# Reordering a batched attention and maxout kernel: the second input batch ahead of the weights, and G pieces formed in the iteration that uses them

## The chip, the cores and the metric

The kernel runs on one core of one Trainium2 chip. The metric is the device time of one execution in microseconds (us). On one core a run counts as slow when it is over 1.5% above the fastest of the same kernel on that chip; such runs are left out of the ratios (with an exception, told at its place). Ratios here are the mean time of one kernel's fast runs over that of the other's fast runs of the same rounds, so they are not quite the ratio of the medians that stand beside them. Where 95% intervals are given, they belong to those ratios.

## The reference

A cross attention between 8 batches of x (8 heads, 512 rows of 64) and a small state (32 rows of 64), in both directions, feeds a maxout layer. All inputs are float32.

```python
def _attn_ref(x, state):
    scale = 1.0 / np.sqrt(D)
    a = softmax(scale * x @ state.T)            # 512 x 32 per head (max and 1e-09 left out here)
    xread = a @ state
    a2 = softmax(scale * state @ x.T)           # 32 x 512 per head
    sread = a2 @ x
    return np.concatenate([xread, sread], axis=2)

def _moe_ref(x, w1, w2, w3, w_out):             # x: 4352 x 512 here, w: 512 x 768, w_out: 768 x 512
    h = np.maximum(np.maximum(x @ w1, x @ w2), x @ w3)
    return h @ w_out
```

(The five lines of softmax are shortened to words.) Since xread @ w equals a @ (state @ w), the kernel forms G = state @ W for each batch once, in six column pieces, and multiplies the attention by G: a batch's maxout m needs piece m of G.

## The kernel before

Batches, pieces and maxouts are counted from 0. TensorE works in the program's order, so where a call stands in the text is where its matmuls stand on the engine, and the traces list them in that order. All PSUM (the matmuls' output memory) is held by two rotating sets: four one-bank buffers with the tag "pw", and two two-bank buffers with the tag "two", which scores and G pieces share. The third user of "two" in a row waits until the first user's reader is done.

```python
pp = ctx.enter_context(tc.tile_pool(name="pp", bufs=2, space=bass.MemoryType.PSUM))
# ...
def scores(b, g0, g1):
    if n == 2: p = pp.tile([128, J, n, HS, Ns], F32, tag="two", name="ps")   # whole batch
    else:      p = pp.tile([128, J, n, HS, Ns], F32, tag="pw", bufs=4, name="psh")
    # ... 16 (or 8) matmuls into p
    nc.scalar.activation(out=e[b][:, :, g0:g1], in_=p, func=AF.Exp, scale=scale)

def softmax(b, g0, g1, mul):      # VectorE: sum, reciprocal; mul: product, on VectorE or GpSimd
# ...
def a_transpose_dma(b):           # transposed attention aT by a DMA
    nc.sync.dma_start_transpose(out=aT[b]..., in_=a[b]...)

def g_cols(b, ms, copies=(nc.scalar.copy, nc.scalar.copy), defer=(False, False)):
    for m, copy, wait in zip(ms, copies, defer):
        p = pp.tile([128, 2, 512], F32, tag="two", name="pg")
        # ... 8 matmuls of state and W into p, then copy p into G[b]

def maxout(b, m, n, lhs, rhs, nk):
    for i in range(3):
        p = pp.tile([128, 512], F32, tag="pw", bufs=4, name=f"pw{i}")   # 2 matmuls each
    # ...
    nc.scalar.copy(out=t0[:, 0:n], in_=pw[0][:, 0:n])                   # "t" on ScalarE
    nc.vector.tensor_max(t1[:, 0:n], t0[:, 0:n], pw[1][:, 0:n])
    nc.vector.tensor_max(ht[b][:, m, :], t1[:, 0:n], pw[2][:, 0:n])

def ffn_out(b, j):                # output block: 6 matmuls into a "pw" buffer, copied by ScalarE
```

W is loaded by GpSimd's queue in four chunks (pieces 0, 1, 2 and 3, 4 and 5), each of three loads (w1, w2, w3). The loads are issued by the same engine that computes one of the softmax products. The loop, with the next batch n = b + 1 prepared behind the maxouts of batch b (cut):

```python
for b in range(2, B):
    if n < B:
        slots[0].append(lambda: scores(n, 0, 2))
        slots[1].append(lambda: softmax(n, 0, 2, nc.gpsimd.tensor_mul))
        slots[1].append(lambda: g_cols(n, (0, 1)))
        slots[2].append(lambda: a_transpose_dma(n))
        slots[3].append(lambda: sread(n))
        slots[3].append(lambda: g_cols(n, (2, 3)))
        slots[5].append(lambda: g_cols(n, (4, 5)))
        # ... and, every other batch, the states of two later batches: a transposing DMA, GpSimd copies
    for m in (1, 2, 4, 5):
        if pending: slots[m].append(lambda t=pending.pop(0): ffn_out(*t))
    for m in range(NM):
        x_maxout(b, m)
        for f in slots[m]: f()
```

Of the kernel before, what the change touches and what calls it, by code (L numbers as in the profile page):

```python
# [15 lines left out]
def kernel(  # L16
# [68 lines left out]
    for b in range(B):  # L85
        nc.gpsimd.memset(x_sb[b][:, XW:XW + D], 1.0)
# [5 lines left out]
    def load_w(c):  # L92
        m0, m1 = chunks[c]
        for i, w in enumerate((moe_w1, moe_w2, moe_w3)):
            nc.gpsimd.dma_start(  # L95
                out=w_sb[c][:, :, i, :],
                in_=w.rearrange("(kk p) f -> p kk f", p=128)[:, :, m0 * 128:m1 * 128])
# [6 lines left out]
    load_w(0)  # L104
    bds = [data.tile([128, 2, H, 2, Ns], BF16, name=f"bd{k}") for k in range(B // 2)]
    nc.vector.memset(bds[0], 0.0)
    load_x(1)
    load_w(1)
# [215 lines left out]
    both = (True, True)  # L324
# [11 lines left out]
    load_w(2)  # L336
    scores(0, 1, 2)
    softmax(0, 1, 2, nc.vector.tensor_mul)
    g_cols(0, (0,))
    load_w(3)  # L340
    load_x(2)
    keep_busy(4)
    a_transpose(0, 0, act)
    a_transpose(0, 1, dve)
    load_st(1, nc.scalar)
    x_maxout(0, 0)
    x_transpose(1, 0, act)
    x_transpose(1, 1, dve)
    sread(0)
    scores(1, 0, 2)  # L350
    softmax(1, 0, 2, nc.vector.tensor_mul)
# [3 lines left out]
    load_x(3)  # L355
    states_cast(1, pool)
    g_cols(0, (1,))
    g_cols(1, (0,), defer=both)
    x_maxout(0, 1)
    a_transpose(1, 0, act)  # L360
    a_transpose(1, 1, dve)
    g_cols(0, (2, 3), (act, dve))
    x_maxout(1, 0)
    x_maxout(0, 2)
    g_cols(1, (1, 2), defer=both)
    x_maxout(0, 3)
# [3 lines left out]
    x_maxout(1, 1)  # L370
    g_cols(0, (4, 5), defer=both)
    x_maxout(1, 2)
    scores(2, 0, 2)
    softmax(2, 0, 2, nc.gpsimd.tensor_mul)
    a_transpose_dma(2)
    x_transpose_dma(3)
    x_maxout(0, 4)
    g_cols(1, (3, 4), defer=both)
    sread(1)
    x_maxout(0, 5)  # L380
    g_cols(1, (5,))
    g_cols(2, (0,), defer=both)
    x_maxout(1, 3)
    ffn_out(0, 0)
    g_cols(2, (1, 2), (act, dve), defer=both)
    x_maxout(1, 4)
# [5 lines left out]
    g_cols(2, (3, 4))  # L392
    sread(2)
    ffn_out(0, 2)
    g_cols(2, (5,))
# [3 lines left out]
    pending = [(1, j) for j in range(J)]  # L399
    for b in range(2, B):  # L400
        n = b + 1
        slots = [[] for _ in range(NM)]
        if n < B:
            slots[0].append(lambda: scores(n, 0, 2))
            slots[1].append(lambda: softmax(n, 0, 2, nc.gpsimd.tensor_mul))
            slots[1].append(lambda: g_cols(n, (0, 1)))
            slots[2].append(lambda: a_transpose_dma(n))
            slots[3].append(lambda: sread(n))
            slots[3].append(lambda: g_cols(n, (2, 3)))
            slots[5].append(lambda: g_cols(n, (4, 5)))  # L410
            slots[4].append(late_transposes)
            if n + 1 < B:
                slots[0].append(lambda: x_transpose_dma(n + 1))
            if n % 2 and n + 1 < B:
                slots[2].append(lambda: states((n + 1) // 2, pool))
            if n + 2 < B:
                slots[0].append(lambda: load_x(n + 2))
        else:
            for m in range(NM):
                slots[m].append(lambda m=m: s_maxout(m))  # L420
        for m in (1, 2, 4, 5):
            if pending:
                slots[m].append(lambda t=pending.pop(0): ffn_out(*t))
        for m in range(NM):
            x_maxout(b, m)
            for f in slots[m]:
                f()
        pending += [(b, j) for j in range(J)]
    assert pending == [(B - 1, j) for j in range(J)]
# [36 lines left out]
```

## Time and profile before

| | before |
|---|---|
| median of the first 3 runs | 165.56 us (164.5 to 165.8) |
| span of the profiled run | 161.6 us |
| score of batch 3 starts (the loop's first) | 51.52 us |
| scores of batches 4 to 7 | 67.23, 82.94, 98.64, 114.72 us |
| first maxout of batch 2 starts | 50.22 us |

The scores are a good clock for the loop: they come once in a batch, so the distance of two is the loop's period (15.71 us), and what lies ahead of the first is the start. The page and the chain are shown in the prediction. Here are three lines of TensorE's waits; a line reads: the engine and the line that waited, what it waited for, then us in total, how many times, and the longest.

```profile
PE pg L249 <- ACT G L255: 2.3, 4, 0.8
...
PE pg L249 <- ACT e L181: 0.8, 1, 0.8
...
PE pg L249 <- DMA w<-in_moe_w_dram: 0.5, 1, 0.5
```

All of these lie in the start. W is hardly waited for (0.5 us), and the wait of a G piece for the exponential ("ACT e") happened once.

### The profile page before, as it was taken

Reading aid. Unit: us, or ns where it says so; the run is one execution under the profiler, and the core shown is the slowest. Engines: PE = TensorE matmul, PEld = TensorE weight load, DVE = VectorE, ACT = ScalarE, POOL = GpSimd, SP = SyncE. Lnnn points to the kernel's source line nnn. Section 1 sums busy time; section 2 is a strip of 40 time slices with the busy share of each in tenths; the row PEclk is TensorE's granted clock in tenths of the full one; section 3 lists DMA queues with packets and bytes.
Section 4 is the critical chain, followed back from the end, with each engine's and each line's share of the span. In section 5 each row is a group of like instructions: output and inputs, shape, how many; then the busy total and the mean of one; then the engine's idle time right before and its main releaser. Section 6 shows DMA issues by size and latency. Waiting matters only on the chain.

```text
span 161.6 us, 3531 instructions
## 1 busy us (share of the span) xinstructions
PE 149.4 (92%) x1417; PEld 70.8 (44%) x1417; DVE 95.8 (59%) x160; ACT 95.6 (59%) x153; POOL 48.0 (30%) x69
## 2 busy tenths in 40 slices
PE   7669799688999999999999999999999999999990
PEld 2336245243445443544344434443444366666440
DVE  4775788576572775576548663956394665585001
ACT  3354667758666936884687667675767653333440
POOL 8979520013063044606031334240123010100140
PEclk9999789999999999999999999999999999999999
DMA  4999999907739995599969639342305230030365
GB/s 120 206 166 195 197 197 211 204 6 38 163 130 132 185 219 106 186 197 231 176 185 139 57 73 274 119 111 94 134 0 154 53 130 2 0 130 4 130 218 171
DMA packets 37873, 21.99 MB, mean 136 GB/s; under 512 B 23009, under 2 KB 35553, under 8 KB 37857
## 3 DMA queue, kind: packets, MB, share of 16 engines
q0 software_dynamic: 17168, 14.94, 47.9%
q1 hardware_dynamic: 20400, 6.56, 22.0%
q10 hardware_dynamic: 288, 0.26, 0.6%
q8 instruction: 11, 0.18, 0.5%
q14 instruction: 6, 0.04, 0.1%
HBM read 15.20 MB, written 8.91 MB: 149 GB/s over the span
## 4 chain that ended last, share of the span: by engine, by line
PE 81%; ACT 8%; DVE 3%; DMA 3%; issue 2%; POOL 1%; SPq 0%; ACTq 0%; DVEq 0%; POOLq 0%
PE pw L270 41%; PE po L295 28%; PE pg L249 6%; ACT G L255 3%; DMA x0f<-in_x_dram 3%; PE psr L221 2%; ACT t L274 2%; PE ps L176 2%; ACT e L181 1%; DVE ht L278 1%; DVE xT L158 1%; PE pat L202 1%; POOL a L191 1%; ACT bd L139 0%; DVE x L331 0%
## 5 line engine op out<-in xcount | busy, mean ns | idle before, releaser
L270 PE MATMUL pw<-aT,G 128*128 128x512 bf16 x288 | 71.7, 384 | 0.9 <-DVE ht L278 0.5
L277 DVE TENSOR_TENSOR t<-t,pw 128x512 bf16<-128x512 bf16 (+1 forms) x54 | 35.1, 651 | 40.6 <-ACT t L274 37.2
L295 PE MATMUL po<-wout,ht 128*128 128x512 bf16 x204 | 48.7, 380 | 0.0
L270 PEld LDWEIGHTS <-G 128*128 128x128 bf16 x288 | 26.9, 98 | 34.5 <-issue 5.7
L255 ACT CAST G<-pg 128x768 bf16<-128x768 f32 x46 | 35.1, 803 | 10.4 <-PE pg L249 10.0
L278 DVE TENSOR_TENSOR ht<-t,pw 128x512 bf16<-128x512 bf16 (+1 forms) x54 | 35.5, 658 | 6.0 <-PE po L295 0.5
L274 ACT CAST t<-pw 128x512 bf16<-128x512 f32 (+1 forms) x54 | 30.6, 566 | 12.8 <-PE pw L270 11.4
L306 ACT COPY osb<-po 128x512 f32<-128x512 f32 x33 | 19.3, 586 | 25.5 <-PE po L295 25.2
L295 PEld LDWEIGHTS <-ht 128*128 128x128 bf16 x204 | 19.0, 98 | 23.8 <-issue 3.3
L315 POOL DMA_DIRECT2D out_dram<-osb x14 | 7.9, 566 | 55.0 <-ACT osb L306 54.3
L191 POOL TENSOR_TENSOR a<-e,rden 128x1024 bf16<-128x1024 bf16 (+1 forms) x7 | 12.5, 1784 | 38.2 <-DVE rden L190 29.1
L249 PE MATMUL pg<-w,bd 64*32 64x384 bf16 x384 | 13.5, 331 | 3.6 <-ACT G L255 2.3
L188 DVE TENSOR_REDUCE den<-e 128x32 f32<-128x1024 bf16 (+1 forms) x9 | 9.8, 1090 | 2.8 <-ACT e L181 2.8
L181 ACT ACTIVATE e<-ps 128x1024 bf16<-128x1024 f32 x7 | 7.2, 1024 | 5.4 <-PE ps L176 5.4
L249 PEld LDWEIGHTS <-bd 64*32 64x32 bf16 x384 | 3.9, 89 | 12.6 <-issue 11.2
L95 POOL DMA_DIRECT2D w<-in_moe_w_dram x12 | 9.0, 772 | 0.0
L270 PE MATMUL pw<-ats,w 128*128 128x256 bf16 x72 | 8.8, 273 | 0.0
L270 PEld LDWEIGHTS <-w 128*128 128x128 bf16 x72 | 7.0, 98 | 2.1
L139 POOL COPY bd<-stT 64x512 bf16<-64x512 bf16 x4 | 4.3, 1078 | 9.5 <-DMA stT<-st 9.4
L70 POOL DMA_DIRECT2D x<-in_x_dram x7 | 6.6, 944 | 1.5 <-DMA w<-in_moe_w_dram 1.2
L176 PEld LDWEIGHTS <-xT 128*128 128x128 bf16 x128 | 4.8, 98 | 3.4 <-DVE xT L158 1.0
L117 PE MATMUL idle<-zero 128*128 128x512 bf16 x13 | 4.6, 490 | 1.2 <-DVE zero L81 1.2
(43 smaller groups left out, 61.3 us busy)
## 6 DMA issues: line engine op xcount, KB each, us to landing
out_dram<-osb POOLq DMA_DIRECT2D x14, 512.0 KB, 3.4
x<-in_x_dram POOLq DMA_DIRECT2D x7, 512.0 KB, 7.4
w<-in_moe_w_dram POOLq DMA_DIRECT2D x6, 256.0 KB, 7.7
w<-in_moe_w_dram POOLq DMA_DIRECT2D x6, 128.0 KB, 5.5
wout<-in_moe_w_out_dram POOLq DMA_DIRECT2D x1, 768.0 KB, 14.1
x0f<-in_x_dram SPq DMA_DIRECT2D x1, 512.0 KB, 4.1
out_dram<-osb SPq DMA_DIRECT2D x1, 512.0 KB, 2.7
x<-in_x_dram POOLq DMA_DIRECT2D x1, 256.0 KB, 5.0
```

The costliest lines, as they stand in the source:

```text
L95: nc.gpsimd.dma_start(out=w_sb[c][:, :, i, :], in_=w.rearrange("(kk p) f -> p kk f", p=128)[:, :, m0 * 128:m1 * 128])
L181: nc.scalar.activation(out=e[b][:, :, g0:g1], in_=p, func=AF.Exp, scale=scale)
L188: nc.vector.reduce_sum(out=den, in_=e[b][:, :, g0:g1], axis=AX.X)
L191: mul(out=a[b][:, :, g0:g1].rearrange("p j g s n -> p j (g s) n"), in0=e[b][:, :, g0:g1].rearrange("p j g s n -> p j (g s) n"), in1=rden.r ...
L249: nc.tensor.matmul(p[32 * s:32 * s + 32, g, 0:384].rearrange("p (i f) -> p i f", i=3), bd(b, 2 * s + g)[64 * g:64 * g + 64, g, :], w[64 * ...
L255: copy(out=G[b][:, :, m * 384:(m + 1) * 384], in_=p[:, :, 0:384])
L270: nc.tensor.matmul(p[:, 0:n], lhs(i, k), rhs(k), start=(k == 0), stop=(k == nk - 1))
L274: nc.scalar.copy(out=t0[:, 0:n], in_=pw[0][:, 0:n])
L277: nc.vector.tensor_max(t1[:, 0:n], t0[:, 0:n], pw[1][:, 0:n])
L278: nc.vector.tensor_max(ht[b][:, m, :], t1[:, 0:n], pw[2][:, 0:n])
L295: nc.tensor.matmul(p, ht[b][:, m, j * 128:(j + 1) * 128], wout_sb[:, m, :], start=(m == 0), stop=(m == NM - 1))
L306: act(out=o[:, j, :], in_=p)
```

## The change

Its intent: fill the holes of the start by giving TensorE a second batch to work on early (x of batch 1 ahead of W, and its attention beside that of batch 0), and form pieces 2 to 5 of a batch's G in its own iteration rather than one iteration ahead. The diff, cut to its core:

```diff
-    for b in range(B):
-        nc.gpsimd.memset(x_sb[b][:, XW:XW + D], 1.0)
+    load_x(1)
 ...
     load_w(0)
+    load_w(1, (0,))
-    load_x(1)
-    load_w(1)
 ...
     softmax(0, 0, 1, nc.gpsimd.tensor_mul)
-    load_w(2)
+    load_w(1, (1, 2))
     scores(0, 1, 2)
     softmax(0, 1, 2, nc.vector.tensor_mul)
+    x_transpose(1, 0, act)
+    x_transpose(1, 1, dve)
     a_transpose(0, 0, act)
     a_transpose(0, 1, dve)
+    g_cols(0, (0,))
+    scores(1, 0, 1)
+    scores(1, 1, 2)
+    softmax(1, 0, 1, nc.gpsimd.tensor_mul)
+    load_w(2)
+    softmax(1, 1, 2, nc.vector.tensor_mul)
+    load_w(3)
 ...   # maxouts of batches 0 and 1 in another mix; then:
+    x_maxout(1, 3)
     scores(2, 0, 2)
+    ffn_out(0, 0)
+    x_maxout(1, 4)
+    softmax(2, 0, 2, nc.gpsimd.tensor_mul)
+    a_transpose_dma(2)
     ffn_out(0, 1)
     x_maxout(1, 5)
     sread(2)
+    g_cols(2, (0, 1))
     ffn_out(0, 2)
     ffn_out(0, 3)
 ...   # the loop
-            slots[1].append(lambda: g_cols(n, (0, 1)))
-            slots[3].append(lambda: sread(n))
-            slots[3].append(lambda: g_cols(n, (2, 3)))
-            slots[5].append(lambda: g_cols(n, (4, 5)))
+        slots[0].append(lambda: g_cols(b, (2, 3), (act, dve)))
+        slots[2].append(lambda: g_cols(b, (4, 5)))
+        if n < B:
+            slots[4].append(lambda: sread(n))
+            slots[4].append(lambda: g_cols(n, (0, 1)))
+        for j, m in enumerate((1, 2, 4, 5)):
+            slots[m].insert(0, lambda j=j: ffn_out(b - 1, j))
```

In slot 0 the G pieces stand right behind the score of the next batch; in slot 2 the output block comes first, and the G pieces stand right ahead of maxout 3.

More of the change, by code (lines that the diff above doesn't have):

```diff
@@ L90, with load_w @@
     wout_sb = wpool.tile([128, NM, d_model], BF16, name="wout")
-    def load_w(c):
+    def load_w(c, parts=(0, 1, 2)):
         m0, m1 = chunks[c]
-        for i, w in enumerate((moe_w1, moe_w2, moe_w3)):
+        for i in parts:
+            w = (moe_w1, moe_w2, moe_w3)[i]
             nc.gpsimd.dma_start(
@@ L104 @@
     load_w(0)
+    for b in range(B):
+        nc.gpsimd.memset(x_sb[b][:, XW:XW + D], 1.0)
+    load_w(1, (0,))
     bds = [data.tile([128, 2, H, 2, Ns], BF16, name=f"bd{k}") for k in range(B // 2)]
     nc.vector.memset(bds[0], 0.0)
-    load_x(1)
-    load_w(1)
     warm = const.tile([128, 1], F32, name="warm")
@@ L322, in late_transposes @@
             late.pop(0)()
-    both = (True, True)
     keep_busy(5)
@@ L335 @@
     softmax(0, 0, 1, nc.gpsimd.tensor_mul)
-    load_w(2)
+    load_w(1, (1, 2))
     scores(0, 1, 2)
     softmax(0, 1, 2, nc.vector.tensor_mul)
-    g_cols(0, (0,))
-    load_w(3)
-    load_x(2)
     keep_busy(4)
+    x_transpose(1, 0, act)
+    x_transpose(1, 1, dve)
     a_transpose(0, 0, act)
     a_transpose(0, 1, dve)
-    load_st(1, nc.scalar)
+    g_cols(0, (0,))
[5 more added lines that the diff above has]
+    load_w(3)
+    load_st(1, nc.gpsimd)
+    load_x(2)
     x_maxout(0, 0)
-    x_transpose(1, 0, act)
-    x_transpose(1, 1, dve)
+    g_cols(0, (1,))
+    g_cols(1, (0,))
     sread(0)
-    scores(1, 0, 2)
-    softmax(1, 0, 2, nc.vector.tensor_mul)
+    a_transpose(1, 0, act)
+    a_transpose(1, 1, dve)
+    x_maxout(0, 1)
     nc.gpsimd.dma_start(out=wout_sb, in_=moe_w_out.rearrange("(kk p) f -> p kk f", p=128))
@@ L355 @@
     load_x(3)
-    states_cast(1, pool)
-    g_cols(0, (1,))
-    g_cols(1, (0,), defer=both)
-    x_maxout(0, 1)
-    a_transpose(1, 0, act)
-    a_transpose(1, 1, dve)
-    g_cols(0, (2, 3), (act, dve))
-    x_maxout(1, 0)
-    x_maxout(0, 2)
-    g_cols(1, (1, 2), defer=both)
-    x_maxout(0, 3)
+    x_maxout(1, 0)
+    g_cols(0, (2, 3), (act, dve))
+    sread(1)
+    g_cols(1, (1,), defer=(True,))
+    x_maxout(0, 2)
+    x_maxout(1, 1)
+    g_cols(1, (2, 3), defer=(False, True))
+    x_maxout(0, 3)
+    states_cast(1, pool)
+    g_cols(0, (4, 5), defer=(False, True))
+    x_maxout(1, 2)
+    x_maxout(0, 4)
     states(1, act)
@@ L369 @@
     x_transpose(2, 1, act)
-    x_maxout(1, 1)
-    g_cols(0, (4, 5), defer=both)
-    x_maxout(1, 2)
+    x_maxout(0, 5)
+    g_cols(1, (4, 5), defer=(False, True))
+    x_maxout(1, 3)
+    x_transpose_dma(3)
     scores(2, 0, 2)
+    ffn_out(0, 0)
+    x_maxout(1, 4)
     softmax(2, 0, 2, nc.gpsimd.tensor_mul)
     a_transpose_dma(2)
-    x_transpose_dma(3)
-    x_maxout(0, 4)
-    g_cols(1, (3, 4), defer=both)
-    sread(1)
-    x_maxout(0, 5)
-    g_cols(1, (5,))
-    g_cols(2, (0,), defer=both)
-    x_maxout(1, 3)
-    ffn_out(0, 0)
-    g_cols(2, (1, 2), (act, dve), defer=both)
-    x_maxout(1, 4)
     ffn_out(0, 1)
@@ L391 @@
     x_maxout(1, 5)
-    g_cols(2, (3, 4))
     sread(2)
+    g_cols(2, (0, 1))
     ffn_out(0, 2)
-    g_cols(2, (5,))
     ffn_out(0, 3)
-    pending = [(1, j) for j in range(J)]
     for b in range(2, B):
@@ L403 @@
         if n < B:
+            if n + 1 < B:
+                slots[0].append(lambda: x_transpose_dma(n + 1))
             slots[0].append(lambda: scores(n, 0, 2))
             slots[1].append(lambda: softmax(n, 0, 2, nc.gpsimd.tensor_mul))
-            slots[1].append(lambda: g_cols(n, (0, 1)))
             slots[2].append(lambda: a_transpose_dma(n))
-            slots[3].append(lambda: sread(n))
-            slots[3].append(lambda: g_cols(n, (2, 3)))
-            slots[5].append(lambda: g_cols(n, (4, 5)))
-            slots[4].append(late_transposes)
-            if n + 1 < B:
-                slots[0].append(lambda: x_transpose_dma(n + 1))
             if n % 2 and n + 1 < B:
                 slots[2].append(lambda: states((n + 1) // 2, pool))
+            slots[5].append(late_transposes)
             if n + 2 < B:
@@ L420 @@
                 slots[m].append(lambda m=m: s_maxout(m))
-        for m in (1, 2, 4, 5):
-            if pending:
-                slots[m].append(lambda t=pending.pop(0): ffn_out(*t))
+        slots[0].append(lambda: g_cols(b, (2, 3), (act, dve)))
[5 more added lines that the diff above has]
+            slots[m].insert(0, lambda j=j: ffn_out(b - 1, j))
         for m in range(NM):
@@ L427 @@
                 f()
-        pending += [(b, j) for j in range(J)]
-    assert pending == [(B - 1, j) for j in range(J)]
     ffn_out(B - 1, 0)
```

## The prediction

> **What bounds the kernel now.** I read the page's shares first, then the span in 40 slices, then the chain that ended last, then the timeline around two places in it.
>
> ```profile
> PE 149.4 (92%) x1417; PEld 70.8 (44%) x1417; DVE 95.8 (59%) x160; ACT 95.6 (59%) x153; POOL 48.0 (30%) x69
> ...
> PE   7669799688999999999999999999999999999990
> ...
> PEclk9999789999999999999999999999999999999999
> ```
>
> TensorE is the bound on average, but the slices (4.04 us each) show two stages. Up to about 40 us TensorE has holes: in the stretches 0-10, 10-20, 20-30 and 30-40 us it is busy 6.90, 7.87, 9.09 and 7.92 us, so 8.2 us of the 40 are empty, and one stretch ran at a reduced clock (0.7 and 0.8 in slices 4 and 5). From 40 us to the end it is full. The chain says the same: until 39.15 us it jumps between DMA, VectorE, ScalarE and TensorE, and from there it is TensorE alone, save one 1.1 us step at 110 us. One batch of the steady loop, score to score:
>
> ```profile
> 67.39 0.47 PE ps L176 x16
> 67.86 1.29 PE pw L270 x6
> 69.15 0.45 PE pg L249 x16
> 69.60 1.40 PE po L295 x6
> ...
> 83.10 0.47 PE ps L176 x16
> ```
>
> The columns are start, length, what. The period is 83.10 - 67.39 = 15.71 us, and its TensorE pieces add up to that: six maxouts (pw) and four output blocks (po) of 1.29 us, three pairs of G pieces (pg) of 0.45, a score (0.47), a state read (0.56), and 0.07 to 0.11 at each change of shape. So in the loop any new wait of TensorE is lost one for one, and only the first 40 us have something to win.
>
> **What the Trainium skill says.** "PSUM — Partial Sum Buffer", Specifications (TRN2): eight banks of 2 KiB per partition. The kernel's two pools take four one-bank buffers ("pw": maxouts, output blocks, state reads, transposes) and two two-bank buffers ("two": scores and G pieces), all eight; a score and two G pieces therefore compete for two buffers. "Perfetto Trace Analysis", Identifying Performance Opportunities (Optimization Strategy): "Consistent bubbles" on the engine that should be saturated "can mean there isn't enough SBUF/PSUM for the next tile to be allocated". The trace before has it once, at 15 us:
>
> ```profile
> 14.98 0.90 PE L176 MATMUL ps<-bd,xT 128*128 128x64 bf16 x16
> ...
> 15.82 0.36 PE L249 MATMUL pg<-w,bd 64*32 64x384 bf16 x8
> 15.93 1.02 ACT L181 ACTIVATE e<-ps 128x1024 bf16<-128x1024 f32 x1 [1.00 <-PE ps L176]
> ...
> 17.00 0.36 PE L249 MATMUL pg<-w,bd 64*32 64x384 bf16 x8 [0.83 <-ACT e L181]
> ```
>
> A score and two G pieces in a row: the second G piece needs the score's buffer and stood 0.83 us until the exponential had read it. "ScalarE: Activation LUTs", What ACT_TABLE_LOAD costs: an ACTIVATE takes 186 ns + 0.833 ns per element with an immediate scale, and back-to-back ones overlap by about 93 ns. The trace agrees: 1.02 us for the exponential of 1024 elements (1.04 by the formula), 0.80 for one G copy of 768, and 1.50 for two in a row. "TensorE: Matmul & The Clock Gate", Part 1: the gate is at half or full clock, by windows of about 3.4 us; the dip in slices 4 and 5 fits, behind a poorly filled stretch.
>
> **The change, part by part.** The matmuls are the same; only places change. I read the order of the built programs engine by engine, with their waits.
>
> *Loop, score and G pieces.* Before: maxout 0, score of the next batch, maxout 1, then two G pieces. After: maxout 0, score, G pieces 2 and 3 at once. The changed program has on the second of them a wait for ScalarE, that of the 15 us case. Worked with the loop's durations: in the batch at 67.23 us the exponential starts 0.72 us after the score (67.95) and ends at +1.74; the second piece can start at about +1.79; TensorE gets there at 0.46 (score, start to start) + 0.23 (half a pair) = +0.69. Loss 1.10 us in each of the five iterations that still score a next batch (b = 2 to 6): 5.5 us. The 15 us case had 0.83, which would make 4.2.
>
> *Loop, G pieces 4 and 5.* After, they come right ahead of maxout 3, which is followed by maxout 4 with no output block between. Both copies are on ScalarE ahead of maxout 3's first copy (t). The like of it before, where an output block did follow and hid it:
>
> ```profile
> 75.38 0.52 PE L249 MATMUL pg<-w,bd 64*32 64x384 bf16 x16
> ...
> 75.81 1.50 ACT L255 CAST G<-pg 128x768 bf16<-128x768 f32 x2 [1.10 <-PE pg L249]
> 75.83 0.98 PEld L270 LDWEIGHTS <-G 128*128 128x128 bf16 x6 [0.31 <-issue]
> 75.83 1.47 PE L270 MATMUL pw<-aT,G 128*128 128x512 bf16 x6
> ...
> 77.19 0.60 ACT L274 CAST t<-pw 128x512 bf16<-128x512 f32 x1
> ```
>
> Here t started 1.36 us after its maxout and ended at +1.96, against +0.68 and +1.27 when no G copy is ahead (65.93, 66.61). After, the output block's copy is ahead too: it starts 0.20 after the G matmuls, then 0.48 for it and 2 x 0.69 for the two G copies, so t starts 2.06 and ends 2.65 after the G matmuls began, 2.20 after maxout 3 did. By the waits, maxout 4's second product needs t's buffer, and its third the one that VectorE's first max frees (+0.04, 0.69 long, +0.04: +2.97). TensorE is ready for the second at 1.40 + 0.43 = 1.83, stands 0.37 to 0.41, is ready for the third at 2.67 and stands 0.30. Loss 0.71, five times 3.6 us. In b = 7 the state maxout lies between; I put 0.45.
>
> *Loop, taken away.* Waits of 0.07 us beside pairs, about 0.4 in all.
>
> *Start.* x of batch 1 now lands ahead of W. In the 40 finer slices of the DMA view for 0-45 us the transfers move some 0.2 MB per us (176 to 210 GB/s); counted in bytes as they land, x1 is then 1.44 MB into the stream, about 9.4 us (before, its transposes ran at 13.27), and the first W piece 1.83 MB, about 11.4 (before, G waited for it until 8.92). The first transposed attention was only there at 10.7, and the first maxout began at 11.81. I walked the engines by hand with the rows' durations (0.69 us per VectorE max, 0.59 per ScalarE copy, 0.7 to 0.8 per G copy, 1.29 per maxout): first maxout 12.9 us, since VectorE now does batch 1's softmax ahead of its two maxes, which end at 17.5; the second waits for those buffers until 17.0; two of its successors follow by 19.8; then G pieces 2 and 3 stand until about 21.2 for the third W chunk, because GpSimd issues it only after the product for batch 1 at 15.4 (before it was issued from 10.63). From there maxouts of both batches alternate, VectorE paces them at about 1.4 us each, and the last output block of batch 0 ends at about 45.2 us. Before, the same work, with four G pieces of batch 2 (0.9 us) on top, ended at 50.39. That would be a gain of 50.39 - 0.9 - 45.2 = 4.3 us.
>
> But batch 2's softmax was moved behind maxout (1,4): sum 40.5, reciprocal to 42.0, GpSimd product (1.91) to 43.9, then the transposing DMA, 4.7 us from issue to landing for this batch before (issued at 37.76, long ahead of its use at 50.39). So maxout (2,0) starts at about 48.5: 3.3 us are given back, and 1.0 stays.
>
> **Sum.** 5.5 + 3.6 + 0.45 - 0.4 - 1.0 = +8.1 us; 165.56 + 8.1 = 173.7. The walk of the start is the loosest term and the 0.83 case says that the first could be 1.3 smaller, so I put 173.0.
>
> **Rivals.** (1) The start gains its full 4 us or more and the attention of batch 2 arrives in time, since GpSimd's and VectorE's places may fall earlier than my walk has them. For it: before, 8.2 us of holes lie there, and filling them is the change's intent. Against it: the softmax's place in VectorE's order is fixed behind ten maxouts' maxes. With full loop losses: 165.56 + 9.1 - 4.3 = 170.4. (2) Moving G pieces costs nothing, as TensorE's waits are covered: then only the start counts, 161 to 165. For it: ScalarE and VectorE are only 59% busy. Against it: the wait for the exponential is one of latency, seen at 0.83 us with ScalarE free. (3) The loop becomes ScalarE- or VectorE-bound: ScalarE has per batch 6 x 0.59 + 5 x 0.7 + 4 x 0.59 + 1.02 = 10.4 us, VectorE 12 x 0.69 + 2.0 of softmax and state read + 0.96 = 11.2, both well below 17.5, so no. (4) The start is worse: the 3.3 us hole and the thin stretch at 14-17 us let the clock gate close for a window or two more, each up to 1.7 us: 175 to 177.
>
> **Range and chances.** The loop losses are read off waits in the program and have a case in the trace: 6 to 10 us. The start is -4.5 to +2. Together 169.0 to 177.0. Within 2% (up to 168.9) asks for the smallest loss and the largest gain at once; faster asks for rival 2. Slower by over 2%: 0.88, within: 0.10, faster: 0.02.
>
> **What would show it.** Right: the loop's period, score to score, at about 17.5 instead of 15.71 us; on the G matmul a recurrent wait of about 1 us for the exponential, five times; waits of 0.3 to 0.4 on the maxout after pieces 4 and 5, for ScalarE's t and VectorE's max; batch 1's transposes at 9 to 10 us; maxout (2,0) waiting about 3 us for the transposing DMA. Wrong: a period below 16.2 us, or maxout (2,0) beginning before 46 us with no wait.

## The result

The changed kernel takes 179.4 us in the median of 4 runs (179.01 to 181.7), the kernel before 165.68 in 4 runs beside it (164.5 to 169.08). The ratio is 1.0876, with an interval of 1.0789 to 1.0963. The direction was right; the size was not: 173.0 was predicted, and 179.4 lies above the range of 169 to 177.

The page after (shares and instructions of the engines; then TensorE's busy tenths and granted clock in 40 slices of 4.4 us):

```profile
PE 153.0 (86%) x1397; PEld 72.2 (41%) x1417; DVE 100.9 (57%) x167; ACT 91.6 (52%) x149; POOL 49.6 (28%) x71
...
PE   7877549999947798979898999899899999999991
...
PEclk9999966999996999999999999999999999999999
```

TensorE's share fell from 92% to 86%. There are two things to see. Counted from 0, slices 4 and 5 are thin and so are 11 to 13, both with a reduced clock beside them. And from slice 14 to 28 there are 8s and 7s where before there was an unbroken 9. TensorE's waits name all of it:

```profile
PE pg L250 <- DMA w<-in_moe_w_dram: 4.4, 2, 4.1
PE pg L250 <- ACT e L182: 4.4, 5, 0.9
PE pw L271 <- DMA aT<-a: 3.6, 1, 3.6
PE pw L271 <- ACT t L275: 1.4, 5, 0.3
```

Two of these come five times, once for each iteration that still scores a next batch; two come in the start. I take the loop first. The chain that ended last, one batch from score to score (start, length, what):

```profile
74.69 0.48 PE ps L177 x16
75.25 1.03 ACT e L182
...
84.00 0.50 ACT t L275
84.52 0.70 DVE t L278
85.26 0.59 PE pw L271 x2
...
92.21 0.48 PE ps L177 x16
```

The period is 92.21 - 74.69 = 17.52 us, and the exponential, ScalarE's copy t and VectorE's first max of it have become links of the chain. The timeline of that batch (start, length, engine, line, operation, in brackets the idle time before it and what ended it):

```profile
75.25 1.02 ACT L182 ACTIVATE e<-ps 128x1024 bf16<-128x1024 f32 x1 [0.81 <-PE ps L177]
...
76.33 0.35 PE L250 MATMUL pg<-w,bd 64*32 64x384 bf16 x8 [0.89 <-ACT e L182]
...
82.49 1.51 ACT L256 CAST G<-pg 128x768 bf16<-128x768 f32 x2
...
83.87 1.11 ACT L275 CAST t<-pw 128x512 bf16<-128x512 f32 x2
...
84.54 1.31 PE L271 MATMUL pw<-aT,G 128*128 128x512 bf16 x4 [0.29 <-ACT t L275]
```

The second G piece starts at 76.33, just after the exponential that read the score has ended at 76.27. Maxout 4's second product (the x4 row at 84.54) stood 0.29 us until the first of the two t copies, that of maxout 3, was through, and that copy comes on the chain only at 84.00, where both G copies have ended (82.49 + 1.51). Its third product could have followed after the 0.43 us of the second, at 84.97; by the chain it started at 85.26, when VectorE's first max had ended.

In the start, TensorE's timeline:

```profile
9.86 1.07 PE L156 MATMUL pxt<-ident,x 128*128 128x128 bf16 x16 [0.49 <-DMA x<-in_x_dram]
...
24.49 0.84 PE L250 MATMUL pg<-w,bd 64*32 64x384 bf16 x16 [4.10 <-DMA w<-in_moe_w_dram]
...
54.20 2.72 PE L271 MATMUL pw<-aT,G 128*128 128x512 bf16 x6 [3.59 <-DMA aT<-a]
```

The first line is the intent fulfilled: x of batch 1 is transposed at 9.86 us, where before it was 13.27. The second is the G pieces 2 and 3 of batch 0, 4.10 us late for their W; they took 0.84 us instead of 0.52, and the maxout of batch 2 took 2.72 instead of 1.47: both ran at half clock (granted clock 0.50 from 24.5 to 26.7 and from 54.2 to 57.0 us). The timeline of GpSimd and of the SyncE queue says where those waits come from:

```profile
16.04 4.52 POOL L95 DMA_DIRECT2D w<-in_moe_w_dram  x6
...
47.31 1.91 POOL L192 TENSOR_TENSOR a<-e,rden 128x1024 bf16<-128x1024 bf16 x1 [17.95 <-DVE rden L191]
...
49.25 1.23 SPq L208 DMA_TRANSPOSE aT<-a  x1
```

W's third and fourth chunk are issued from 16.04 us on, since the program puts GpSimd's softmax product for batch 1 ahead of them. Before it was:

```profile
10.63 4.52 POOL L95 DMA_DIRECT2D w<-in_moe_w_dram  x6
```

Batch 2's product ends at 49.22, so that its transposing DMA lands only at 54.07.

The scores of batches 3 to 7 start at 56.72, 74.53, 92.05, 109.57 and 127.09 us. Between the two profiled spans, 161.6 and 177.4, there are 15.8 us: 5.20 come ahead of the first of these scores (56.72 against 51.52), and 10.63 behind it (120.68 to the end against 110.05). The medians differ by 13.7, because the profiled run of before, at 163.36 us, was faster than the median of its runs.

### The profile page after: what moved, and what is told of

It reads as the page before. It is cut to its first block, busy times and chain, and to the rows that moved or that the text cites. A ratio compares the mean times of both kernels' runs of the same rounds, so it can differ in the third digit from the quotient of the medians.

```text
span 177.4 us, 3523 instructions
## 1 busy us (share of the span) xinstructions
PE 153.0 (86%) x1397; PEld 72.2 (41%) x1417; DVE 100.9 (57%) x167; ACT 91.6 (52%) x149; POOL 49.6 (28%) x71
## 4 chain that ended last, share of the span: by engine, by line
PE 61%; ACT 11%; DMA 11%; DVE 6%; issue 5%; POOL 5%; ACTq 0%; POOLq 0%; DVEq 0%
PE pw L271 31%; PE po L296 21%; DMA w<-in_moe_w_dram 8%; PE pg L250 4%; ACT G L256 4%; ACT e L182 3%; DVE t L278 3%; DMA aT<-a 3%; ACT t L275 2%; PE psr L222 2%; PE ps L177 2%; POOL a L192 2%; POOL w L95 2%; ACT osb L307 1%; DVE ht L279 1%
## 5 line engine op out<-in xcount | busy, mean ns | idle before, releaser
L271 PE MATMUL pw<-aT,G 128*128 128x512 bf16 x288 | 74.0, 391 | 6.3 <-DMA aT<-a 3.6
L278 DVE TENSOR_TENSOR t<-t,pw 128x512 bf16<-128x512 bf16 (+1 forms) x54 | 35.1, 650 | 43.9 <-ACT t L275 34.7
L296 PE MATMUL po<-wout,ht 128*128 128x512 bf16 x184 | 46.6, 379 | 0.7
L256 ACT CAST G<-pg 128x768 bf16<-128x768 f32 x41 | 31.4, 804 | 11.0 <-PE pg L250 11.0
L296 PEld LDWEIGHTS <-ht 128*128 128x128 bf16 x204 | 19.8, 98 | 23.7 <-issue 0.3
L192 POOL TENSOR_TENSOR a<-e,rden 128x1024 bf16<-128x1024 bf16 (+1 forms) x8 | 13.5, 1690 | 56.2 <-DVE rden L191 44.5
L250 PE MATMUL pg<-w,bd 64*32 64x384 bf16 x384 | 14.3, 340 | 9.2 <-DMA w<-in_moe_w_dram 4.4
L256 DVE CAST G<-pg 128x768 bf16<-128x768 f32 x7 | 6.7, 957 | 8.5 <-PE pg L250 8.5
L250 PEld LDWEIGHTS <-bd 64*32 64x32 bf16 x384 | 4.0, 89 | 16.6 <-issue 15.8
L182 ACT ACTIVATE e<-ps 128x1024 bf16<-128x1024 f32 x6 | 6.1, 1024 | 5.2 <-PE ps L177 5.1
L118 PE MATMUL idle<-zero 128*128 128x512 bf16 x13 | 5.3, 554 | 1.2 <-DVE zero L81 1.2
```

The costliest lines, as they stand in the source:

```text
L192: mul(out=a[b][:, :, g0:g1].rearrange("p j g s n -> p j (g s) n"), in0=e[b][:, :, g0:g1].rearrange("p j g s n -> p j (g s) n"), in1=rden.r ...
L250: nc.tensor.matmul(p[32 * s:32 * s + 32, g, 0:384].rearrange("p (i f) -> p i f", i=3), bd(b, 2 * s + g)[64 * g:64 * g + 64, g, :], w[64 * ...
L256: copy(out=G[b][:, :, m * 384:(m + 1) * 384], in_=p[:, :, 0:384])
L271: nc.tensor.matmul(p[:, 0:n], lhs(i, k), rhs(k), start=(k == 0), stop=(k == nk - 1))
L296: nc.tensor.matmul(p, ht[b][:, m, j * 128:(j + 1) * 128], wout_sb[:, m, :], start=(m == 0), stop=(m == NM - 1))
```

## The experiments

My theory: the loop's two waits and the start's two waits make the whole loss, and each can be removed by moving a call. The rivals: the loop is slow for some other reason, such as G being formed late at all; the start costs what it does because of the low clock and not because of the waits; or behind a removed wait the next one stands at once. The edits below are against the changed kernel. The ratio against before is what can be compared.

| run | what it is | median us | ratio to before, 95% |
|---|---|---|---|
| a_oldloop | start of after, loop of before | 169.48 | 1.0340 (1.0262 to 1.0418) |
| b_oldstart | start of before, loop of after | 173.47 | 1.0581 (1.0509 to 1.0654) |
| c_w2early | third W chunk issued earlier | 173.95 | 1.0598 (1.0510 to 1.0685) |
| d_soft2early | softmax of batch 2 earlier | 174.0 | 1.0624 (1.0524 to 1.0725) |
| e_g23late / e_again | pieces 2, 3 behind maxout 1 | 175.17 / 174.73 | 1.0738 (1.0636 to 1.0840) / 1.0634 (1.0566 to 1.0701) |
| f_g45early / f_again | pieces 4, 5 ahead of the output block | 176.7 / 174.53 | 1.0769 (1.0677 to 1.0861) / 1.0607 (1.0524 to 1.0690) |
| g_all | c, d, e and f | 162.83 | 0.9937 (0.9867 to 1.0007) |
| h_busy / h_again | TensorE kept busy in both gaps | 178.28 / 178.54 | 1.0886 (1.0795 to 1.0977) / 1.0861 (1.0790 to 1.0932) |
| after_again | after, unedited | 179.82 | 1.0860 (1.0758 to 1.0963) |
| j_states0 | g_all, states earlier | 169.9 | 1.0275 (1.0183 to 1.0368) |
| k_oldstart_fixed | b with e and f | 164.9 | 1.0032 (0.9962 to 1.0102) |
| n_w3late | a gap between W chunks 3 and 4 | one look, 178.37 | state unknown |
| p_stsplit | g_all, states' DMA earlier | 161.56 | 0.9862 (0.9802 to 0.9922) |

### The two halves: a_oldloop and b_oldstart

The first undoes the loop, the second the start. The four G pieces of batch 2 that change sides were put where the loop needs them.

```diff
 # a_oldloop: start kept; loop of before, and
     ffn_out(0, 2)
+    g_cols(2, (2, 3))
     ffn_out(0, 3)
+    g_cols(2, (4, 5))
 # b_oldstart: everything ahead of the loop as before, but of batch 2 only pieces 0 and 1
-    g_cols(2, (1, 2), (act, dve), defer=both)
+    g_cols(2, (1,), (act,), defer=(True,))
 ...
-    g_cols(2, (3, 4))
-    g_cols(2, (5,))
```

(The second diff is against the kernel before.)

> Start of the changed kernel, loop of the kernel before (all of G formed an iteration ahead; batch 2's four later pieces behind its last output blocks, where TensorE waits anyway). Theory (start and loop are two separate losses, read off the two profiles: from the score in batch 2's iteration to the end 120.5 us after and 109.9 before): 179.4 - 10.6 = 168.8 us, period 15.7. Rival (the loop's loss comes with the late start, not with its order): above 175 us.

> Start of the kernel before without batch 2's G pieces 2 to 5, loop of the changed kernel. Theory: 165.6 + 10.6 - 0.9 (four pieces fewer in the start) = 175.3 us, period 17.5, the five waits for the exponential there. Rival (the loop's loss needs the new start): under 170 us.

The start alone costs 3.4%, the loop alone 5.8%; the sum, 9.2%, is close to the whole change's 8.8%. So the halves are nearly independent. In b the loop's period was 17.5 us (scores at 51.24, 68.71 and 86.23) at full clock, so the loop's loss needs neither the new start nor a low clock. In a, TensorE's waits for W (4.6 us) and for the transposed attention (3.0) stayed, and the last two periods are those of the kernel before, 15.71 us (88.94, 104.65, 120.36).

### The start's two waits: c_w2early and d_soft2early

```diff
 # c_w2early
     load_w(1, (1, 2))
+    load_w(2)
     scores(0, 1, 2)
 ...
     softmax(1, 0, 1, nc.gpsimd.tensor_mul)
-    load_w(2)
 # d_soft2early
     scores(2, 0, 2)
+    softmax(2, 0, 2, nc.gpsimd.tensor_mul)
+    a_transpose_dma(2)
     ffn_out(0, 0)
     x_maxout(1, 4)
-    softmax(2, 0, 2, nc.gpsimd.tensor_mul)
-    a_transpose_dma(2)
```

> Changed kernel, with the third W chunk's three loads issued ahead of GpSimd's product for batch 1. Theory (the place of the issue makes G pieces 2 and 3 of batch 0 stand 4.1 us, and the standing closes the clock gate): the wait falls to under 1 us and the half clock at 21 to 28 us goes with it, some 5 to 6.5 us, 173 to 174.4 us. Rival 1 (only the wait): 175.3 us with the half clock still there. Rival 2 (the transfers themselves are too slow, whenever issued): no change, 179 us.

> Changed kernel, with batch 2's softmax and its transposing DMA right behind its score, ahead of output block 0 and maxout (1,4). Theory (the wait of 3.6 us for the transposing DMA and the half clock after it come of the softmax's place): GpSimd's product starts at about 44.5 instead of 47.3, wait under 1 us, no half clock in batch 2: 179.4 - 3 - 1.7 = 174.7 us. Rival (VectorE's sum ahead of maxout (1,4) holds up TensorE as much as it gains): 177 to 179 us.

Each gained some 2.5% against the unedited 1.086 and 1.0876. The kernel before was 2.3 us faster than beside the unedited kernel, so the expected microseconds have to be read as ratios: c's 1.0598 lies between its theory (1.049 to 1.057) and its rival 1 (1.063), and its interval takes in both; d's 1.0624 is close to its theory (1.059). TensorE's timeline, first of c and then of d:

```profile
22.04 0.52 PE L250 MATMUL pg<-w,bd 64*32 64x384 bf16 x16
```

```profile
48.98 1.46 PE L271 MATMUL pw<-aT,G 128*128 128x512 bf16 x6 [0.92 <-DMA aT<-a]
```

In c the pieces 2 and 3 started at 22.04 us with no wait for W and at full clock (1.00 from 20 to 32 us, as the theory has it), while the wait for aT stayed at 3.6 us (its profile fell into a slow run of 177.32 us, so I read from it only the waits and this stretch). In d that wait fell from 3.6 to 0.9 us: the product started at 42.09 instead of 47.31, and the maxout of batch 2 at 48.98 instead of 54.20, with no half clock there. GpSimd had stood 17.95 us for this product, so only the place of the call held it back.

### The loop's two waits: e_g23late and f_g45early, each run twice

```diff
 # e: in the loop
-        slots[0].append(lambda: g_cols(b, (2, 3), (act, dve)))
 ...
             slots[m].insert(0, lambda j=j: ffn_out(b - 1, j))
+        slots[1].insert(0, lambda: g_cols(b, (2, 3), (act, dve)))
 # f: in the loop
-        slots[2].append(lambda: g_cols(b, (4, 5)))
 ...
             slots[m].insert(0, lambda j=j: ffn_out(b - 1, j))
+        slots[2].insert(0, lambda: g_cols(b, (4, 5)))   # ahead of the output block
```

In e maxout 1 runs while the exponential reads the score; in f the output block runs while the G pieces are copied.

> Changed kernel, with G pieces 2 and 3 of a batch moved from behind the next batch's score to behind maxout 1 (ahead of its output block). Theory (the second piece needs the score's PSUM buffer and waits for the exponential, 1.1 us in each of five iterations, nothing else there costs): the wait of pg for the exponential is gone, the period falls from 17.52 to 16.4 us, total -5.5 us, ratio to before 1.0876 - 0.033 = 1.054. Rival (the wait only moves: maxout 2 now waits for the copies of G, which come later): period stays above 17.2, ratio above 1.08.

> Changed kernel, with G pieces 4 and 5 moved from right ahead of maxout 3 to ahead of the output block before it. Theory (ScalarE's two G copies hold up the first copy of maxout 3, and so the PSUM buffers of maxout 4, for 0.71 us in five iterations and about 0.45 in the last): the waits of pw for ScalarE's t go, period 16.8 us, total -4.0 us, ratio about 1.063. Rival (VectorE's pace in two maxouts in a row makes the wait, whatever is ahead): under 1 us gained, ratio above 1.081.

The first pair gained less in time than expected, and the profiled execution of f ran at a granted clock of 0.659 throughout (227.9 us). So both were run again:

> The edit of e_g23late again (G pieces 2 and 3 behind maxout 1). Its profile showed the period at 16.4 to 16.8 us, its timed runs gained only 2.3 us. Theory (the loop's term is 5 times 0.9 to 1.1 us, and the start's scatter hid it): ratio 1.055 to 1.062 against 1.086 to 1.0876 unedited. Rival (a gain in the loop is lost elsewhere): 1.07 or above again, and the profile shows where.

> The edit of f_g45early again (G pieces 4 and 5 ahead of the output block), whose only profile fell into a run at 0.66 of the clock. Theory (0.71 us in five iterations, 0.45 in the last): no wait of pw for ScalarE's t, period 16.8, ratio 1.062 to 1.066. Rival (some 2 us, as the first three runs had it): 1.072 to 1.077, period 17.1 to 17.3.

The timeline of TensorE, first of e_again and then of f_again:

```profile
72.51 0.63 PE L177 MATMUL ps<-bd,xT 128*128 128x64 bf16 x16
...
74.36 0.52 PE L250 MATMUL pg<-w,bd 64*32 64x384 bf16 x16
```

```profile
79.20 2.75 PE L271 MATMUL pw<-aT,G 128*128 128x512 bf16 x12
```

In e both G pieces now run in one stretch of 0.52 us with nothing to wait for; in f maxouts 3 and 4 run through in 2.75. The clean periods were 72.51 to 88.95 = 16.44 us in e and 71.37 to 88.15 = 16.78 in f, against 17.52: 1.08 and 0.74 us less, where the prediction has 1.10 and 0.71. The times moved by 2.3% and 2.5% against the unedited kernel in the second pair, and by 1.2% and 0.9% in the first, where five waits of that size would make 3.3% and 2.3% of some 164 us. In the first pair e cannot be judged: its three timed runs (174.94 to 177.24) are all marked slow beside the profiled 171.61, and the ratio is the mean of these three; the one run marked fast would give 1.048. So f gave what was expected in the second pair only, and e fell short in the second. A part of that is in the profile: each edit brought one new wait of a score for GpSimd's state copies, of 0.59 and 0.75 us. The rest of it I have no run for.

### All four edits: g_all

> All four edits at once: third W chunk early, batch 2's softmax early, G pieces 2 and 3 behind maxout 1, G pieces 4 and 5 ahead of the output block. Theory (the four losses are separate and add): the ratios 1.0598 and 1.0624 of the first two runs and -0.033 and -0.024 for the others make 1.0876 - 0.028 - 0.025 - 0.033 - 0.024 = 0.978, period 15.7 us: faster than the kernel before by 2%. Rival (they share one wait, so that mending one opens another): 1.00 to 1.03.

It ran at 0.9937, between the theory's 0.978 and the rival's 1.00: with the four waits gone the loss is gone (the interval reaches 1.0007, and the clean periods are 15.71 us as before), but no clear gain over before remains. The start does gain: the score of batch 3 begins at 48.16 us, against 51.52 before, of which 0.9 are the G pieces that moved behind it. One of TensorE's new waits takes back a part:

```profile
PE ps L177 <- POOL bd L140: 1.3, 2, 1.2
```

GpSimd copies the states of later batches into place (bd) after a transposing DMA; the loop is now fast enough for the score to arrive before them. A second, of 1.2 us, was for x of batch 1 at the very start.

### Keeping the clock up: h_busy, and again as h_again

```diff
     x_maxout(1, 0)
+    keep_busy(18)
     g_cols(0, (2, 3), (act, dve))
 ...
     ffn_out(0, 3)
+    keep_busy(15)
```

These are idle matmuls into a "two" buffer in both gaps of the start. If the low clock costs time, filling the gaps should gain it, as long as nothing else moves.

> Changed kernel, with matmuls on zeros put where TensorE stands: 18 ahead of G pieces 2 and 3 of batch 0 (3.9 us at full clock), 15 ahead of batch 2's first maxout (3.2 us). The waits stay, only their filling changes. Theory (standing closes the clock gate, and the half clock of 6.8 and 3.4 us behind the two waits costs 0.5 us per us of work in it, some 3 to 4 us): clock 1.0 behind both waits, ratio about 1.066. Rival (the waits alone are the loss, or the gate follows something else): ratio 1.08 to 1.09.

> The run that fills TensorE's standing with matmuls on zeros, again: its clock was 1.0 and its time not better, while its one profile had the transposing DMA land 1.3 us later than all others. Theory (that was chance; the half clock does cost time): ratio 1.066 to 1.076. Rival (the clock is off the path that sets the end, or the fill costs what it gains): 1.083 to 1.09 again.

The clock was full, but no time was gained: 1.0886 and 1.0861 against 1.0876 and 1.0860. Here is the 20-30 us stretch of both (stretch, length, then busy us and count of TensorE, its weight loads, VectorE, ScalarE and GpSimd, granted clock, DMA share, GB/s), first of after:

```profile
20.00:30.00 10.00, 5.90 (x66) 2.23 (x65) 4.19 (x8) 2.24 (x4) 5.45 (x8) 0.66 1.37 191
```

and of h_again:

```profile
20.00:30.00 10.00, 8.23 (x87) 3.65 (x87) 4.57 (x9) 2.67 (x4) 5.53 (x8) 1.00 1.35 186
```

In h_again's trace the full clock did shorten what it touches: from G pieces 2 and 3 to the score of batch 2 it took 15.19 us instead of 16.77, and from the maxout of batch 2 to the score of batch 3 1.30 instead of 2.52, together 2.8 us less. But those G pieces started 1.5 us later (25.97 against 24.49): 0.6 of it because x of batch 1 had landed later, which happened ahead of any filler, and most of the rest because W took 9.25 us from the first issue to the G pieces instead of 8.45. And the transposing DMA for batch 2 took 6.16 us (49.15 to 55.31, where the maxout began), where it took 4.8 to 5.0 in every run of the new start without filler; h_busy's took 6.15. So in this trace the gain was eaten by transfers. I have no run that shows why they were slower. For the transposing DMA there is a candidate: the DMA view from 47 to 57 us of h_again has a line that no trace of the new start without filler (13 of them) has between this DMA's issue and its landing, and h_busy's has it too:

```profile
q8 instruction: 1, 0.02, 0.6%
```

This is one packet of the queue that the profile calls instruction. In both runs there are also some 1.5 us in this time in which all transfers together moved at most 14 GB/s. The fillers lengthen the program and may have brought this packet to this place; that is not shown, and in the kernel before, with such a packet at the same place, the DMA took 4.7 us.

How much time the half clock costs in the changed kernel is therefore not shown by the runs' times. The traces show a part: from the start of G pieces 2 and 3 to that of the score of batch 2, c_w2early took 15.03 us at full clock and h_again 15.02, against 16.61 in after, and in c the maxout of batch 2 came 28.13 us behind these pieces instead of 29.71. So the 1.6 us behind the first gap do reach batch 2's maxout. The second gap does not always lower the clock: in f_again the wait for aT was 3.61 us, and the maxout took 1.46. Of the six unedited runs of after_again, two took 177.26 and 177.89 us at a mean clock of 0.989 and 0.978, and four took 179.72 to 180.19 at 0.961 to 0.979. That fits a cost of about 2 us, but it is a correlation, and the one at 0.979 with 180.08 us is against it.

> The changed kernel itself, unedited, to have it beside the kernel before on the chip of the edited ones. Both theories: ratio 1.080 to 1.095. If it is near 1.089, filling TensorE's standing with matmuls gained nothing in all; if near 1.095 or above, it gained.

This run repeated the result: 1.0860 against 1.0876.

### Why the W loads came late: n_w3late

Here GpSimd writes a dummy tile eight times (4.6 us) between the third and the fourth W chunk, so that the third chunk's loads are alone in the queue.

```diff
     softmax(1, 1, 2, nc.vector.tensor_mul)
+    pad = const.tile([128, 512], BF16, name="pad")
+    for _ in range(8):
+        nc.gpsimd.memset(pad, 0.0)
     load_w(3)
```

> Changed kernel, with eight idle memsets on GpSimd (some 3 us in all) between the loads of the third and the fourth W chunk. Why did the third chunk land at 24.4 us and not at 21.2 as predicted? Theory (its last part shares the DMA engines with the fourth chunk's loads, issued right behind): it lands 1 to 1.5 us sooner, G pieces 2 and 3 start at about 23.2 us. Rival (the transfers only start slowly after standing from 15 to 17.5 us, and take turns in order): no change, 24.4 us.

It is one look at 178.37 us, of unknown state, and is used for its durations only. The timeline of GpSimd and TensorE in it:

```profile
17.03 2.29 POOL L95 DMA_DIRECT2D w<-in_moe_w_dram  x3
...
24.12 0.52 PE L250 MATMUL pg<-w,bd 64*32 64x384 bf16 x16 [2.73 <-DMA w<-in_moe_w_dram]
```

From the first issue to the G pieces it took 24.12 - 17.03 = 7.1 us, against 24.49 - 16.04 = 8.45 in after. The single loads took 4.1, 4.7 and 5.4 us from issue to landing, against 4.4, 4.9 and 6.8. By the clock the pieces came at 24.12, close to the rival's 24.4, but only because the issue was 1.0 us later. The shorter time fits the theory, yet it does not show that sharing makes the difference: e_g23late, whose start is unedited and whose fourth chunk follows at once, took 7.05 us (16.20 to 23.25), and the ten traces that issue both chunks in a row lie anywhere from 7.05 to 9.25. What makes this spread stays open. What all of them share is a slow start. The DMA view of after from 15 to 27 us, in slices of 0.3 us, shows their start:

```profile
GB/s 0 0 0 55 0 0 0 0 22 32 58 96 148 191 198 196 191 203 195 171 121 123 130 145 186 178 183 166 169 172 183 191 188 196 190 198 195 200 222 324
```

The loads begin in the slice at 17.4 us and reach the rate of the full queue only at 18.9, some 2.9 us after GpSimd began to issue them. With 0.79 MB at 0.2 MB per us, 3.9 us, that makes some 6.8 us (an estimate), about the shortest of the times above.

### Forming G late, by itself: k_oldstart_fixed

This is b_oldstart with the loop edits e and f, so that of the change only the place where G is formed is left.

> Start of the kernel before (without batch 2's G pieces 2 to 5), loop of the changed kernel with its two G pairs moved as in the two runs that did so. Theory (forming G within the iteration is neutral once the two waits are gone): 1.0581 - 0.033 - 0.024 = 1.001, period 15.7 to 15.9. Rival (it is worth something in itself, ScalarE and VectorE being evener): under 0.985.

At 1.0032 it is level with the kernel before: with the two pairs moved, forming pieces 2 to 5 in a batch's own iteration costs nothing that can be seen. Whether it would gain something is not shown, since the score waits for GpSimd's state copies (2.0 us in two waits, in a profile of a slow run) as in g_all; without them 1.0032 would become some 0.99, an estimate, still short of the rival's 0.985.

### The wait behind the waits: j_states0 and p_stsplit

The state copies consist of a transposing DMA and GpSimd copies behind it. j_states0 moves both from slot 2 to slot 0 of g_all; p_stsplit moves the DMA alone.

```diff
 # j_states0 (on top of g_all)
             slots[0].append(lambda: scores(n, 0, 2))
+            if n % 2 and n + 1 < B:
+                slots[0].append(lambda: states((n + 1) // 2, pool))
 ...
-            if n % 2 and n + 1 < B:
-                slots[2].append(lambda: states((n + 1) // 2, pool))
 # p_stsplit (on top of g_all): states_dma() holds the DMA, states() only the copies, left in slot 2
             slots[0].append(lambda: scores(n, 0, 2))
+            if n % 2 and n + 1 < B:
+                slots[0].append(lambda: states_dma((n + 1) // 2))
```

> All four edits, and the block states of batches 4 to 7 transposed and copied one slot group earlier (behind the score of the odd batch before, not behind maxout 2). Theory (the run with all four edits shows a new wait, score <- GpSimd's copy of the states, 1.3 us in two places, 3.1 us of transposing DMA and 2.1 us of copies on the chain): the wait goes, 1.2 us less: ratio about 0.987. Rival (GpSimd's softmax product now comes behind those copies and delays the next batch's transposing DMA): 0.994 or above, with a wait of maxout for aT.

> All four edits, and of the block states of batches 4 to 7 only the transposing DMA moved ahead of the attention's, with GpSimd's copies left behind its softmax product. Theory (the wait of score for those copies, 1.3 us, came of the DMA's place in its queue alone): wait gone, no wait for aT as in j_states0: ratio 0.985 to 0.99. Rival (GpSimd itself is late): 0.994 or above, the wait still there.

The first edit was a mistake that its rival foresaw. TensorE's largest wait in j_states0:

```profile
PE pw L271 <- DMA aT<-a: 8.7, 4, 4.5
```

GpSimd stood 9.40 us for the states' DMA in front of its copies, and the softmax product of the next batch stood behind them in its order; so the attention came late. With the DMA alone moved, p_stsplit's wait for bd was gone, and TensorE's largest wait was:

```profile
PE pw L276 <- DMA aT<-a: 2.7, 2, 1.8
```

Of these, 0.9 us stood in g_all too; the other 1.8 are new, against the theory, and were not followed up. p_stsplit takes 161.56 us (161.16 to 162.91), at 0.9862 (0.9802 to 0.9922) of the kernel before: less than 2%, but the interval lies below 1. It has the lowest ratio, though its interval overlaps that of g_all, so what the moved DMA alone is worth is not shown. It keeps the whole intent of the change.

## Why the prediction was right or wrong

In short: the loop's terms held. The step that failed is the walk of the start: in it the landing of W's third chunk, put at 21.2 us and seen at 24.4, and the low clock behind two waits, which the sum left out.

- **Loop, score and G pieces: right.** A loss of 1.10 us in five iterations was predicted, with the second piece 1.79 us behind the score; the trace has it 1.80 behind (76.33 - 74.53), with five waits of 0.9 for the exponential, and removing them shortened the period by 1.08. The mechanism, two G pieces behind a score on two shared buffers, is the one that the prediction read from a single place in the trace before.
- **Loop, G pieces 4 and 5: right.** Predicted 0.71, removed 0.74. The waits were 0.29 for t and some 0.3 for VectorE's max in the batch shown, at the two products that the prediction named. Together with the first it makes 17.52 - 15.71 = 1.81 us per batch, which is 1.10 + 0.71.
- **From the score of batch 3 to the end:** 9.1 + 0.45 - 0.4, and 0.9 for the G pieces of batch 2 that moved behind this score, make 10.05 us; 10.63 was measured, with about 0.3 of half clock in the first period.
- **Start, x of batch 1 ahead of W: right.** Transposes at 9.86 (9 to 10 was predicted); the first maxout at 13.37 (12.9).
- **Start, "I walked the engines by hand": this step failed.** It put the score of batch 3 at 48.5 + 1.3 = 49.8 us; it came at 56.72. Of the 6.9 us that are missing:
  - 3.3 us, the largest: G pieces 2 and 3 "stand until about 21.2 for the third W chunk". The order was seen and the issue was on time (16.04, right behind a product that was predicted for 15.4), but the landing was mis-sized. The prediction gives no working for 21.2; it fits 0.79 MB at the 0.2 MB per us of a full queue, 3.9 us. The trace shows 8.45 us from the first issue to the G pieces, and no trace of this order shows less than 7.05, with some 2.9 us until the loads into the empty queue are at full rate; the rest of the 8.45 is open. Before, the queue did not run dry at this point (140 GB/s or more in each slice of 0.3 us from 9 to 20 us), so that trace could not show the time that loads take to get going.
  - 2.0 us: from there to GpSimd's product for batch 2 it took 22.8 us instead of 43.9 - 1.9 - 21.2 = 20.8. Most of it, 1.6 to 1.8 us, is one row of twelve matmuls that took 4.39 us at the low clock instead of about 2.6. In c, without the wait for W, this low clock was gone and with it 1.6 us.
  - 0.4 us: from the product to the maxout of batch 2, 6.9 us instead of 6.5. The place of the softmax behind maxout 4 of batch 1, and the wait of some 3 us for the DMA, were as predicted (3.59).
  - 1.2 us: maxout of batch 2 to score, 2.52 us instead of 1.3, at half clock.
- **Rival 4 named the last terms** (the clock gate closes for a window or two more, 175 to 177 us; its 1.7 us for each is an estimate, half of the window that the prediction cites), and the trace has half clock from 23.2 to 30.0 and from 53.9 to 57.3 us. But the sum did not count them: the holes in my own walk, 3 us at two places, should have been charged with a low clock or at least have widened the range. How much of it a run's time would gain without the low clock is what h_busy and h_again left open.
- **Rivals 1 and 2 fell,** since the start lost rather than gained and the moved pieces cost 1.81 us per batch; rival 3 was rightly ruled out, with ScalarE at 52% and VectorE at 57%.
- **The signs of being wrong did not show:** the period was not below 16.2 us, and the maxout of batch 2 neither came before 46 us nor without a wait. They guarded the mechanisms, which held, and not the length of the walk, which did not.

In numbers, then: 3.3 us of the error are W's landing, 0.4 is the transposing DMA, and 2.8 to 3.0 lie in matmuls that ran at half clock in this trace; the small rest is unassigned. With the 0.6 us behind the score of batch 3 these make up what the two profiled spans have over the predicted sum of 8.1 us (15.8 - 8.1 = 7.7, within 0.2).

## What to carry to other kernels

On an engine that is full, a call right behind one that holds a shared buffer is charged with the latency of that buffer's reader in every iteration. Such a wait can be computed before a run from the buffers' rotation and a few durations (1.81 us per batch here; that the sum fits to the hundredth is luck, since its two parts are off by 0.02 and 0.03), and the cure is to put other work between the two. A transfer into an empty queue must be sized by durations from issue to landing, not by the rate of a full one (here 7.05 to 9.25 us where the rate alone says 3.9), and when an engine both computes and issues transfers, its order decides both. Expect the next wait behind a removed one: here each of the two loop edits, and all four edits together, brought up a wait for state copies that had been hidden.

## What the Trainium skill lacked or had wrong

- "DMA: Bandwidth & Descriptors", Anatomy of one DMA — SWDGE (gpsimd) path: the fit of 2.0 us plus the bytes at 436 GB/s gives, as an estimate, 2.6 us for the 256 KB that a W load writes (3.2 for the 512 KB of float32 that it reads). Alone in the queue the first such load, which converts to bf16, took 4.1 us, and the third of three 5.4. The measurement decides here; the page gives no figure for loads that convert, nor for how three in a row start up.
- The same page, Latency and other measured facts: it has a bandwidth for transposing DMAs (261 GB/s, which would be 1.0 us for the 256 KB of one attention, an estimate), but no time from issue to landing. Here, for batch 2, it was 4.7 to 4.9 us in every run without filler matmuls, and 6.1 in the two with filler, unexplained.
- "TensorE: Matmul & The Clock Gate", Part 1: half clock behind a gap agrees (0.66 in the mean of 20 to 30 us behind a wait of 4.10 us). But keeping the engine busy through such gaps, which follows from the page's rule against idle gaps of more than 3.4 us, gained nothing here (1.0886 and 1.0861 with filler, 1.0876 and 1.0860 without): in h_again's trace the full clock shortened TensorE's work by 2.8 us, and slower transfers took that back. One execution of f_g45early ran at 0.659 for its whole span (227.9 us, where its other runs took 175.69 to 177.4); I found no such state of a lone core on the page.
- "Perfetto Trace Analysis", Identifying Performance Opportunities, was right: "consistent bubbles" were missing buffers, five waits of 0.9 us on the two shared two-bank buffers.
